# Pooled attention and a token and channel mixer on one core: another order of work, 16 heads with a ones column, results scaled on ScalarE

## The chip, the core and the metric

One core of a Trainium2 chip runs the whole program. The metric is the device time of one execution in microseconds; the kernel before has a median of 934.5 us over 3 runs (934.42 to 937.92).

## What is computed

The reference, cut to its core (4 batches, 8 heads, 1152 keys, head size 64; queries are averaged in pairs, so 576 of them):

```python
q_pool = q.reshape(B, H, S // 2, 2, D).mean(axis=3)
scores = 1.0 / np.sqrt(D) * np.matmul(q_pool, k.transpose(0, 1, 3, 2))
attn = np.exp(scores - np.max(scores, axis=-1, keepdims=True))
attn = attn / (np.sum(attn, axis=-1, keepdims=True) + 1e-09)
x = np.matmul(attn, v)                    # heads side by side: (4, 576, 512)
h = np.maximum(x.transpose(0, 2, 1) @ w_tok1, 0.0) @ w_tok2   # token mix, 576 -> 256 -> 576
u = x + h.transpose(0, 2, 1)
out = u + np.maximum(u @ w_ch1, 0.0) @ w_ch2                  # channel mix, 512 -> 1536 -> 512
```

## The kernel before, in words

Precision is kept by splitting each fp32 operand into a high part, rounded to the matmul's fp32r type, and a low part, the rest; products are sums of two or three matmuls. The work has three stages.

**Attention**, head by head, 32 heads. Per pair of heads, keys and pooled queries are loaded and turned by TensorE (`prep_kq`, lines 571 to 644), and copied to high and low tiles KHI, KLO, QHI, QLO. `stack` (lines 657 to 675) then makes, with DMAs from SBUF to SBUF, the stacked operands of a head: QQ holds the high queries twice (two transfers), KK the high keys over the low keys (two transfers, the last from `kl`), and K2 and Q2 the high keys and low queries for the rest of the product, with one more row for the maximum. `maxima` (lines 677 to 729) multiplies QQ by KK, 12 or 15 blocks per head on line 726, and VectorE reduces each block to row maxima on line 728; turned and sent by a small DMA, they become the last row of Q2, so that the score matmuls (line 791) subtract them. `main` (lines 770 to 850) takes nine steps per head: scores into one of two PSUM buffers "s", then ScalarE takes the exponential twice, to fp32 (`pf`, line 803) and to fp32r (`ph`, line 806), and GpSimd or VectorE takes the difference `pl` (line 810). The value matmuls of line 835 multiply ph and pl by V, whose high and low parts stand side by side.

The denominator has two ways. A head in the list `IN_PV` (line 94) has a column of ones next to V's high part, so the sum of the exponentials comes out as a 65th row; that takes three value matmuls per key block and half of the queries instead of two, 18 more per head. Another head has VectorE sum `pf` over the keys in three cuts per half, six per head (line 817), and `finish` turns those sums by five more transposes (line 881) and reduces them (lines 885, 888); it also adds V's two halves (line 848). `finish` (lines 852 to 905) turns the results, takes the reciprocal on VectorE and scales the results into U with two VectorE instructions (lines 900, 903).

**Token mix** per batch and half of the channels (`token_mix`), among the heads that follow. **Channel mix** (`make_ut`, `mm3`, `mm4`) at the end.

The order of each engine's instructions comes from a planner. Each `step` names an engine, a cost in ns, what it reads and writes, and a due time. `Plan.run` (lines 166 to 238) simulates the engines: of all steps that are ready it takes the one that can start first, and among equals the one due first. The order that it finds is the order of issue in the program; on the chip each engine runs its instructions in that order and waits on semaphores. Due times come from the table `DUE` (lines 33 to 91), as offsets in steps of the main loop. All transfers are issued on SP's queue. For them the planner has a common wire: a transfer is on it for its bytes at 360 GB/s (`wire`, line 337), not sooner than 1400 ns after its issue, and ends 900 ns later:

```python
            if s.eng == DMA:
                clock[DMA] = start + 650
                wire = max(start + 1400, wire) + s.cost
                s.end = wire + 900
```

A step with a second engine (`other`, as for pl: GpSimd first, VectorE as the other) is given to the other when the first would end more than `stay` ns later (line 195).

Of the kernel before, what the change touches and what calls it, by code (L numbers as in the profile page):

```python
# [33 lines left out]
    "scores": -1.44,  # L34
    "p_lo": 1.22,
    "sum": -6.47,
    "pv": 2.05,
    "o": -15.19,
    "finish": 7.6,
    "max": -29.13,  # L40
    "max_each": 0.09,
    "prep": -32.24,
    "v": 5.77,
    "stack": 7.14,
    "stack_2": 14.79,
    "mix": 9.79,
    "mix_x": 5.86,
    "w_tok": 0.59,
    "w_tok_each": 7.04,
    "w_bits": -43.21,  # L50
    "sum_each": 2.0,
    "pv_lo": -0.75,
    "lo_first": 70.21,
    "max_first": 50.9,
    "max_second": 0.54,
    "scores_each": -12.27,
    "p_hi": 0.25,
    "pv_one": -0.26,
    "finish_each": -35.22,
    "den_sum": -68.64,  # L60
    "x_lo": 7.7,
    "x": 8.02,
    "den": -16.32,
    "rd": -25.43,
    "u": -61.47,
    "u_each": 32.06,
    "max_of": 6.21,
    "max_row": -89.36,
    "max_first_each": 23.6,
    "q_pool": -42.98,  # L70
    "q_turn": 1.33,
    "k_each": 2.83,
    "k_hi": -30.98,
    "k_lo": 37.53,
    "q_hi": -105.28,
    "q_lo": -23.66,
    "load_kq": -1.52,
    "load_v": -98.6,
    "v_lo": -15.06,
    "load_w_tok": 1.53,  # L80
    "mix_x_lo": -8.66,
    "mix_1": 3.35,
    "mix_t": -0.86,
    "mix_2": 2.41,
    "mix_u": -20.08,
    "w_ch": 22.41,
    "w_ch_each": 12.8,
    "ut_0": -1.45,
    "ut_1": 1.58,
    "stay": 135.0,  # L90
# [3 lines left out]
IN_PV = (0, 1, 2, 3, 4, 5, 7, 9, 11, 12, 13, 15, 16, 18, 19, 21, 22, 23, 25, 27, 28, 31)  # L94
# [15 lines left out]
class Plan:  # L110
# [55 lines left out]
    def run(self):  # L166
# [17 lines left out]
        while len(order) < len(self.steps):  # L184
# [34 lines left out]
            if s.eng == DMA:  # L219
                clock[DMA] = start + 650  # L220
                wire = max(start + 1400, wire) + s.cost
                s.end = wire + 900
            else:
                s.end = clock[s.eng] = start + s.cost
                if s.shared:
                    port = s.end
# [15 lines left out]
def kernel(  # L242
# [24 lines left out]
    P = 128  # L267
# [31 lines left out]
    def f(t):  # L299
        return t.bitcast(F32)  # L300
# [137 lines left out]
    for i in range(2):  # L438
        ve.memset(f(K2[i])[D:D + 1, :], -1.0)
        ve.memset(DEN[i], 1.0)  # L440
    ve.memset(f(MH), 0.0)
    for i in range(2):
        po.memset(f(VV[i])[:, :, P:P + 1], 1.0)
        po.memset(OT[i], 0.0)
# [101 lines left out]
    def load_kq(p, t, after):  # L546
# [24 lines left out]
    def prep_kq(p, t):  # L571
# [10 lines left out]
        def keys(j):  # L582
            ps = Buf("s" if p == 0 else "r")
# [22 lines left out]
        def queries(i):  # L606
            c0, c1 = ((0, 3), (3, 5))[i]
            ps = Buf("s" if p == 0 else "r")
# [21 lines left out]
            if i == 1:  # L630
                for j in range(2):
                    r = slice(j * D, (j + 1) * D)
                    step(ACT, act_ps(REM),
                         lambda ps=ps, r=r, j=j, n=n: sc.copy(
                             QD[p % 2][r, j * REM:(j + 1) * REM], bank(ps)[r, n - REM:n]),
                         tq + 1.1 + due["q_hi"], [ps], [("qd", p % 2, j)])
# [20 lines left out]
    def stack(h, t, t2):  # L657
# [3 lines left out]
        for half, dst, src, n, read in (  # L661
# [3 lines left out]
            step(DMA, wire(4 * D * n),  # L665
# [11 lines left out]
    def maxima(h, t):  # L677
# [23 lines left out]
        step(DMA, 6, lambda: sy.dma_start(row[:, 0:4 * P], mt[0:4]), t,  # L701
             [("mt", h % 2)], [("row", h % 2, c) for c in range(4)])
        if h > 1:
            step(DMA, 6, lambda: sy.dma_start(
# [3 lines left out]
    def maximum(h, c, n, t):  # L708
# [15 lines left out]
        if h == 1 or h == 0 and c > 2:  # L724
            read.append(("m0", 2))
# [11 lines left out]
    def first_maxima(cs, t):  # L737
# [19 lines left out]
        step(PE, len(cs) * TURN, turn, t, [("m0", c) for c in range(cs[-1] + 1)], [ps], [ps])  # L757
# [12 lines left out]
    def main(h, t0):  # L770
# [8 lines left out]
        for s in range(NS):  # L779
# [3 lines left out]
            for i, (fq, c) in enumerate(units):  # L783
# [5 lines left out]
                def scores(st=st, i=i, fq=fq, c=c, terms=terms):  # L789
# [32 lines left out]
            for i, (fq, c) in enumerate(units):  # L822
# [16 lines left out]
                if c == NK - 1:  # L839
# [6 lines left out]
                    step(ACT, 415, lambda o=o, qs=qs: sc.copy(  # L846
# [5 lines left out]
    def finish(h, t):  # L852
# [25 lines left out]
        if not pv:  # L878
# [20 lines left out]
        r = rows(4)  # L899
        step(DVE, dve(4 * D), lambda: ve.tensor_mul(  # L900
            u[:, c0:c0 + 4, col], turned()[:, 0:4, 0:D], rd[:, 0:4].to_broadcast([P, 4, D])),
            t + due["u"], [*keys, ("rd", i2)], [*[("u", b, c, hh) for c in range(4)], *stage])
        step(DVE, 260, lambda: ve.tensor_mul(
            u[r, 8, col], turned()[r, 4, 0:D], rd[r, 4].to_broadcast([REM, D])),
            t + due["u"] + due["u_each"], [*keys, ("rd", i2)], [("u8", b // 2, hh), *stage])
# [282 lines left out]
```

## Time and profile before

| | us |
|---|---|
| median of 3 runs | 934.5 |
| the profiled execution | 931.58 |
| its span, first to last instruction | 929.8 |
| TensorE busy (matmuls) | 883.9 |
| VectorE busy | 635.0 |
| ScalarE busy | 520.4 |
| GpSimd busy | 331.6 |

The first head's work up to its first exponential ends at about 23 us, and the channel mixer fills the time from about 613 us on. A busy time counts the length of each instruction's record, without counting an overlap twice; matmuls follow each other faster than one record is long, so the pace of a row of matmuls is read from a run of them in the chain, not from the mean of one. In the rows below PE is TensorE, PEld its weight loads, DVE VectorE, ACT ScalarE, POOL GpSimd and SPq the issuing of transfers; "out<-in" are tile names with their numbers left out.

### The profile page before, as it was taken

The numbers are of one execution on the slowest core, as the hardware profiler recorded it, in microseconds if no ns is written. First come the engines' busy times: TensorE is split into PE (matmuls) and PEld (weight loads), VectorE is DVE, ScalarE is ACT, GpSimd is POOL, SyncE is SP. The second block draws the span as 40 slices with busy tenths as digits, with TensorE's granted clock in tenths as the row PEclk, the third lists the DMA queues.
The fourth block names the chain that finished last, engine by engine and source line by source line (L and its number), as shares of the span: only waits on it lengthen the run. The fifth ranks groups of instructions, "written<-read, shape, count | busy, mean of one in ns | idle before, by whom it ended". The sixth has DMA issues, their size and how long they took to land.

```text
span 929.8 us, 15513 instructions
## 1 busy us (share of the span) xinstructions
PE 883.9 (95%) x5679; PEld 817.7 (88%) x5679; DVE 635.0 (68%) x1291; ACT 520.4 (56%) x1040; POOL 331.6 (36%) x273
## 2 busy tenths in 40 slices
PE   7999999999999999989999999999999999999997
PEld 5888898888898899988998898989999999999996
DVE  7597888888888889887788998988882222221211
ACT  2878877768778678666777778854431111111110
POOL 2889747276345255374144735420000000000000
PEclk9999999999999999999999999999999999999999
DMA  6966653536546545644463435034420101000001
GB/s 165 257 148 159 155 126 91 128 94 150 135 96 153 135 97 131 142 98 108 100 150 75 107 71 135 24 113 137 137 91 1 69 1 34 1 35 1 35 1 35
DMA packets 89684, 91.09 MB, mean 98 GB/s; under 512 B 43852, under 2 KB 68808, under 8 KB 89608
## 3 DMA queue, kind: packets, MB, share of 16 engines
q1 hardware_dynamic: 89608, 90.09, 39.5%
q8 instruction: 45, 0.74, 0.3%
q14 instruction: 31, 0.25, 0.1%
HBM read 43.25 MB, written 4.72 MB: 52 GB/s over the span
## 4 chain that ended last, share of the span: by engine, by line
PE 71%; DMA 10%; ACT 7%; DVE 6%; SPq 4%; issue 2%; DVEq 0%; ACTq 0%; POOL 0%; POOLq 0%
PE r L1049 16%; PE o L835 13%; PE s L1077 13%; PE s L791 11%; DMA kk<-kl 10%; PE r L726 7%; PE o L1077 3%; ACT pf L803 3%; ACT ph L806 2%; SPq L666 2%; DVE mx L728 2%; PE r L934 2%; PE r L588 1%; PE r L952 1%; PE r L1077 1%
## 5 line engine op out<-in xcount | busy, mean ns | idle before, releaser
L810 POOL TENSOR_TENSOR pl<-pf,ph 128x576 fp32r<-128x576 f32 x170 | 245.4, 1459 | 189.0 <-ACT ph L806 94.0
L803 ACT ACTIVATE pf<-s 128x576 f32<-128x576 f32 x288 | 201.2, 700 | 121.3 <-PE s L791 115.5
L835 PE MATMUL o<-ph,vv 128*64 128x288 f32 (+2 forms) x972 | 211.5, 299 | 1.2 <-ACT ot L842 1.1
L728 DVE TENSOR_REDUCE mx<-r 128x1 f32<-128x384 f32 x384 | 189.2, 547 | 29.7 <-PE r L726 28.8
L806 ACT ACTIVATE ph<-s 128x576 fp32r<-128x576 f32 x288 | 186.7, 649 | 2.0 <-PE s L791 1.2
L791 PE MATMUL s<-qq,kk 128*128 128x288 f32 x574 | 169.4, 306 | 3.4 <-ACT ph L806 3.3
L791 PE MATMUL s<-q,k 65*128 65x288 f32 x576 | 166.2, 299 | 0.2 <-ACT q L760 0.2
L1057 DVE SCALAR_TENSOR_TENSOR h<-r,h 128x384 fp32r<-128x384 f32 x72 | 40.1, 557 | 168.4 <-ACT h L1055 167.8
L726 PE MATMUL r<-kk,qq 128*128 128x384 f32 x372 | 124.8, 352 | 30.5 <-DMA kk<-kl 26.0
L1055 ACT ACTIVATE h<-r 128x384 fp32r<-128x384 f32 x72 | 35.4, 491 | 195.9 <-PE r L1049 195.9
L835 PEld LDWEIGHTS o<-ph,vv 128*64 128x64 f32 (+2 forms) x972 | 136.5, 146 | 6.4 <-ACT ot L842 2.2
L835 PE MATMUL o<-pl,vv 128*65 128x288 f32 (+1 forms) x576 | 140.0, 300 | 0.8 <-POOL pl L810 0.5
L1077 PE MATMUL s<-w,h 128*128 128x512 f32 x504 | 130.9, 394 | 0.0
L791 PEld LDWEIGHTS s<-qq,kk 128*128 128x128 f32 x574 | 109.9, 192 | 9.0 <-ACT ph L806 6.9
L791 PEld LDWEIGHTS s<-q,k 65*128 65x128 f32 x576 | 110.6, 192 | 0.5 <-ACT q L760 0.5
L810 DVE TENSOR_TENSOR pl<-pf,ph 128x576 fp32r<-128x576 f32 x118 | 92.7, 787 | 24.5 <-ACT ph L806 19.5
L1049 PE MATMUL r<-big,w 128*128 128x384 f32 x576 | 108.8, 337 | 0.0
L1077 PEld LDWEIGHTS s<-w,h 128*128 128x128 f32 x504 | 93.4, 188 | 16.6
L1049 PEld LDWEIGHTS r<-big,w 128*128 128x128 f32 x576 | 101.7, 188 | 3.7 <-DVE big L1038 0.2
L726 PEld LDWEIGHTS r<-kk,qq 128*128 128x128 f32 x372 | 69.6, 192 | 39.6 <-issue 23.3
L835 PEld LDWEIGHTS o<-pl,vv 128*65 128x65 f32 (+1 forms) x576 | 83.4, 153 | 3.9 <-POOL pl L810 1.8
L817 DVE TENSOR_REDUCE sum<-pf 128x96 f32<-128x960 f32 x60 | 67.7, 1138 | 0.8 <-ACT pf L803 0.4
(132 smaller groups left out, 1094.5 us busy)
## 6 DMA issues: line engine op xcount, KB each, us to landing
raw<-in_moe_w_ch_dram SPq DMA_DIRECT2D x24, 512.0 KB
kk<-kh SPq DMA_DIRECT2D x32, 288.0 KB
qq<-qh SPq DMA_DIRECT2D x64, 144.0 KB
kk<-kl SPq DMA_DIRECT2D x32, 288.0 KB
vn<-in_v_dram SPq DMA_DIRECT2D x32, 288.0 KB
k<-kk SPq DMA_DIRECT2D x31, 288.0 KB
kn<-in_k_dram SPq DMA_DIRECT2D x30, 288.0 KB
qn<-in_q_dram SPq DMA_DIRECT2D x32, 256.0 KB
```

The costliest lines, as they stand in the source:

```text
L726: step(PE, mm(SP3), lambda ps=ps, w=w, x=x: te.matmul(at(ps)[:, 0:SP3], w, x, start=True, stop=True), t, read, [ps], [ps])
L728: step(DVE, dve(SP3), lambda ps=ps, m=m: ve.tensor_reduce(m, at(ps)[:, 0:SP3], axis=AX.X, op=ALU.max), t + due["max_of"], [ps], [key])
L791: te.matmul(at(st)[:, i, 0:HF], w[:, c * P:(c + 1) * P], x[:, fq * HF:(fq + 1) * HF], start=(n == 0), stop=(n == len(terms) - 1))
L803: step(ACT, act_ps(2 * HF), lambda pf=pf, st=st: sc.activation(pf, at(st)[:, :, 0:HF], AF.Exp, scale=ESC), t, [(st, 0), (st, 1)], [("pf", s)])
L806: step(ACT, act_ps(2 * HF), lambda ph=ph, st=st: sc.activation(at(ph), at(st)[:, :, 0:HF], AF.Exp, scale=ESC), t + due["p_hi"], [(st, 0), ...
L810: both(2 * HF, lambda e, pf=pf, ph=ph, pl=pl: e.tensor_sub(at(pl), pf, f(at(ph))), t + due["p_lo"], [("pf", s), ph], [pl], [pl], on=POOL i ...
L817: step(DVE, 65 + 1.06 * (NK + 1) * HF // CUT, lambda fq=fq, cs=cs: ve.tensor_reduce(SUM[:, fq, cs], PF[:, fq, :, cs].rearrange("p c x i -> ...
L835: lambda o=o, x=x, w=w, m=m, i=i, c=c, new=new, end=end: te.matmul(at(o)[0:m - w], VV[i2][:, c, w:m], at(x)[:, i], start=new, stop=end),
L1049: te.matmul(at(ps)[:, 0:GT], w[:, c], x[:, c], start=(c == 0 and n == 0), stop=(c == NC4 - 1 and n == 2))
L1055: step(ACT, act_ps(GT), lambda: sc.activation(at(h)[:, 0], at(ps)[:, 0:GT], AF.Relu), t, [ps], [h])
L1057: step(DVE, dve(GT), lambda: ve.scalar_tensor_tensor(out=at(h)[:, 1], in0=at(ps)[:, 0:GT], scalar=0.0, in1=f(at(h))[:, 0], op0=ALU.max, op ...
L1077: te.matmul(at(ps), a[:, x * P:(x + 1) * P], w, start=(fi == 0 and m == 0), stop=(fi == NF - 1 and m == 2))
```

## The change

- **Durations of transfers.** The planner's figures for transfers become longer on the wire (factors of 1.3 to 1.85 for the stacked operands and their copies, 1.4 for query loads) with shorter fixed ends (1265 and 650 ns); the small transfers of the maxima count 1 ns of wire, not 6. Two costs of ScalarE steps are changed as well (the small query copy 230, and pf 49 ns dearer where it is written with gaps).
- **The due times** in `DUE` are all others, and `stay` is 800, not 135. The order of nearly every instruction and transfer can differ.
- **`IN_PV`** has 16 heads, not 22. In these heads pf is written contiguously, except in the middle one of the nine steps.
- **Scaling.** The closing results are scaled by ScalarE, five instructions per head with a scale read per partition, where VectorE had two.
- **First head.** The key row of -1 is filled by ScalarE, not VectorE; two GpSimd fills of OT are left out; of its five turns of keys and queries two use the "s" buffers and three the ring "r", where all five used "s". A step of the maxima waits in the plan for the turn of the first three, not for the third of them.

The diff, cut:

```diff
 DUE = {
...
-    "max": -29.13,
+    "max": -26.45,
...
-    "stack": 7.14,
-    "stack_2": 14.79,
+    "stack": 10.93,
+    "stack_2": 29.0,
...
-    "stay": 135.0,
+    "stay": 800,
 }
-IN_PV = (0, 1, 2, 3, 4, 5, 7, 9, 11, 12, 13, 15, 16, 18, 19, 21, 22, 23, 25, 27, 28, 31)
+IN_PV = (0, 1, 2, 3, 5, 8, 10, 13, 15, 19, 21, 24, 26, 28, 29, 31)
...
-                wire = max(start + 1400, wire) + s.cost
-                s.end = wire + 900
+                wire = max(start + 1265, wire) + s.cost
+                s.end = wire + 650
...
-        ve.memset(f(K2[i])[D:D + 1, :], -1.0)
+        sc.activation(K2[i][D:D + 1, :], ident[D:D + 1, 0:1].to_broadcast([1, S]), AF.Copy,
+                      bias=-1.0, scale=0.0)
...
-        po.memset(OT[i], 0.0)
...
-            step(DMA, wire(4 * 2 * n * (c1 - c0) * D), lambda: sy.dma_start(
+            step(DMA, 1.4 * wire(4 * 2 * n * (c1 - c0) * D), lambda: sy.dma_start(
...
-            ps = Buf("s" if p == 0 else "r")
+            ps = Buf("s" if p == 0 and j == 0 else "r")
...
-            ps = Buf("s" if p == 0 else "r")
+            ps = Buf("s" if p == 0 and i == 0 else "r")
...
-            step(DMA, wire(4 * D * n),
+            step(DMA, (1.3 if dst is QQ else 1.8) * wire(4 * D * n),
...
-        step(DMA, wire(4 * D * S), lambda: sy.dma_start(f(K2[h % 2])[0:D], f(KK[i])[0:D]),
+        step(DMA, 1.85 * wire(4 * D * S), lambda: sy.dma_start(f(K2[h % 2])[0:D], f(KK[i])[0:D]),
...
-        step(DMA, wire(4 * D * SQ),
+        step(DMA, 1.7 * wire(4 * D * SQ),
...
-            pf = (PF[:, 0, s].rearrange("p x i -> p i x") if s < NK // 2
-                  else PF[:, :, NK // 2, :, 0] if s == NK // 2
-                  else PF[:, 1, s - NK // 2 - 1].rearrange("p x i -> p i x"))
-            step(ACT, act_ps(2 * HF), lambda pf=pf, st=st: sc.activation(
+            pv = h in IN_PV
+            half, x = (0, s) if s < NK // 2 else (1, s - NK // 2 - 1)
+            near = pv and s != NK // 2
+            pf = (PF[:, :, NK // 2, :, 0] if s == NK // 2
+                  else PF[:, half, x].rearrange("p x i -> p (x i)").rearrange("p (i x) -> p i x", i=2) if near
+                  else PF[:, half, x].rearrange("p x i -> p i x"))
+            step(ACT, act_ps(2 * HF) + (0 if near else 49), lambda pf=pf, st=st: sc.activation(
...
-        step(DVE, dve(4 * D), lambda: ve.tensor_mul(
-            u[:, c0:c0 + 4, col], turned()[:, 0:4, 0:D], rd[:, 0:4].to_broadcast([P, 4, D])),
...
-        step(DVE, 260, lambda: ve.tensor_mul(
-            u[r, 8, col], turned()[r, 4, 0:D], rd[r, 4].to_broadcast([REM, D])),
...
+        for c in range(NQ):
+            r, row, out_ = ((slice(0, P), c0 + c, ("u", b, c, hh)) if c < 4
+                            else (rows(4), 8, ("u8", b // 2, hh)))
+            step(ACT, 230 if c > 3 else 140, lambda c=c, r=r, row=row: sc.mul(
+                u[r, row, col], turned()[r, c, 0:D], rd[r, c]),
+                t + due["u"] + due["u_each"] * (c > 3), [(ps, 0, c), ("rd", i2)], [out_, *stage])
```

## Rows read from the trace of the kernel before

**Rows 1.** Busy time by stage, whole span (columns named in its first line).

```profile
core 0: us, PE busy (x) PEld busy (x) DVE busy (x) ACT busy (x) POOL busy (x), PEclk, DMA share, GB/s
0.00:23.00 23.00, 17.14 (x69) 11.85 (x70) 16.90 (x44) 4.98 (x11) 5.02 (x16) 0.99 0.69 165
23.00:613.00 590.00, 555.59 (x4010) 524.00 (x4009) 497.90 (x1028) 447.04 (x895) 324.81 (x256) 0.99 0.52 122
613.00:929.80 316.80, 311.21 (x1603) 281.83 (x1601) 120.18 (x222) 68.39 (x135) 1.77 (x1) 1.00 0.15 49
```

**Rows 2.** Who waited for whom, whole span: us in total, times, longest us.

```profile
ACT pf L803 <- PE s L791: 115.5, 109, 3.3
...
PE r L726 <- DMA kk<-kl: 26.0, 19, 2.6
...
PEld s L791 <- ACT ph L806: 6.9, 16, 0.8
...
PE r L726 <- DVE mx L728: 2.1, 4, 1.0
```

**Rows 3.** The chain that ended last, in order of time: start us, us, what.

```profile
126.01 0.66 PE r L588 x6
...
130.19 1.06 PE o L835 x8
...
172.04 5.98 DMA kk<-kl
...
470.44 4.07 DMA kk<-kl
```

**Rows 4.** Instructions in order of time, 131 to 146 us, SP and PE.

```profile
136.11 0.54 SPq L666 DMA_DIRECT2D kk<-kl  x1
...
141.74 0.74 PE L726 MATMUL r<-kk,qq 128*128 128x384 f32 x2 [1.83 <-DMA kk<-kl]
```

**Rows 5.** Busy time and granted clock (PEclk) around three stalls, columns as in rows 1.

```profile
142.00:146.00 4.00, 4.00 (x19) 4.00 (x19) 2.98 (x6) 1.74 (x3) 2.04 (x3) 0.57 0.28 78
...
398.00:402.00 4.00, 4.00 (x20) 4.00 (x19) 3.03 (x9) 2.08 (x5) 1.44 (x2) 0.57 0.03 8
...
23.00:27.00 4.00, 4.00 (x20) 3.90 (x19) 3.36 (x8) 3.48 (x6) 3.10 (x3) 0.63 1.24 220
```

**Rows 6.** Groups by line and shape: count, busy us, mean ns, idle before.

```profile
L810 POOL TENSOR_TENSOR pl<-pf,ph 128x576 fp32r<-128x576 f32 x170 | 245.4, 1459 | 189.0 <-ACT ph L806 94.0 <-PE o L835 51.0 <-DMA qq<-qh 13.8
L803 ACT ACTIVATE pf<-s 128x576 f32<-128x576 f32 x288 | 201.2, 700 | 121.3 <-PE s L791 115.5 <-DVE sum L817 3.9
L728 DVE TENSOR_REDUCE mx<-r 128x1 f32<-128x384 f32 x384 | 189.2, 547 | 29.7 <-PE r L726 28.8
L806 ACT ACTIVATE ph<-s 128x576 fp32r<-128x576 f32 x288 | 186.7, 649 | 2.0 <-PE s L791 1.2
...
L810 DVE TENSOR_TENSOR pl<-pf,ph 128x576 fp32r<-128x576 f32 x118 | 92.7, 787 | 24.5 <-ACT ph L806 19.5 <-issue 2.1 <-PE s L791 0.9
...
L817 DVE TENSOR_REDUCE sum<-pf 128x96 f32<-128x960 f32 x60 | 67.7, 1138 | 0.8 <-ACT pf L803 0.4
...
L900 DVE TENSOR_TENSOR u<-r,rd 128x256 f32<-128x256 f32 x32 | 13.4, 418 | 0.4
...
L848 DVE TENSOR_TENSOR ot<-o,low 64x288 f32<-64x288 f32 x20 | 8.9, 446 | 4.9 <-ACT low L846 4.4
...
L903 DVE TENSOR_TENSOR u<-r,rd 64x64 f32<-64x64 f32 x32 | 7.3, 228 | 0.7
...
L885 DVE TENSOR_REDUCE r<-r 128x4 f32<-128x512 f32 x10 | 7.0, 696 | 2.3 <-PE r L881 2.2
...
L634 ACT CAST qd<-r 64x64 fp32r<-64x64 f32 x30 | 6.5, 218 | 0.6 <-DVE ql L638 0.4
```

**Rows 7.** Instructions in order of time, first 24 us, DVE, PE and ACT.

```profile
1.81 1.02 DVE L439 MEMSET k<- 1x1152 f32 x1 [0.28 <-issue]
...
6.60 0.52 PE L614 MATMUL s<-ident,qp 128*128 128x128 f32 x3 [0.49 <-DVE identr L375]
...
7.15 0.48 ACT L628 CAST qh<-s 128x384 fp32r<-128x384 f32 x1 [5.14 <-PE s L614]
```

More of the change, by code (lines that the diff above doesn't have):

```diff
@@ L33 @@
 DUE = {
[L34 to L39, printed above, removed]
-    "max": -29.13,
-    "max_each": 0.09,
-    "prep": -32.24,
-    "v": 5.77,
-    "stack": 7.14,
-    "stack_2": 14.79,
[L46 to L89, printed above, removed]
-    "stay": 135.0,
+    "scores": -2.94,
+    "p_lo": 5.94,
+    "sum": -8.53,
+    "pv": 1.65,
+    "o": -51.23,
+    "finish": 9.59,
+    "max": -26.45,
+    "max_each": 0.91,
+    "prep": -32.39,
+    "v": 3.41,
+    "stack": 10.93,
+    "stack_2": 29.0,
+    "mix": 4.49,
+    "mix_x": 5.65,
+    "w_tok": 9.27,
@@ new lines @@
+    "w_tok_each": 4.51,
+    "w_bits": -133.66,
+    "sum_each": 0.15,
+    "pv_lo": 0.35,
+    "lo_first": -20.44,
+    "max_first": 50.63,
+    "max_second": 6.11,
+    "scores_each": -5.89,
+    "p_hi": -0.31,
+    "pv_one": 0.14,
+    "finish_each": -4.69,
+    "den_sum": -16.19,
+    "x_lo": -25.04,
+    "x": 38.5,
+    "den": -32.79,
+    "rd": -22.19,
+    "u": 15.67,
+    "u_each": -29.42,
+    "max_of": -7.63,
+    "max_row": -47.64,
+    "max_first_each": 17.12,
+    "q_pool": -5.06,
@@ L91 @@
+    "q_turn": 3.94,
+    "k_each": 1.81,
+    "k_hi": -2.71,
+    "k_lo": 5.81,
+    "q_hi": -15.06,
+    "q_lo": 47.2,
+    "load_kq": -51.29,
+    "load_v": -22.47,
+    "v_lo": -60.85,
+    "load_w_tok": -81.39,
+    "mix_x_lo": -54.2,
+    "mix_1": 3.42,
+    "mix_t": 0.6,
+    "mix_2": 3.13,
+    "mix_u": -133.49,
+    "w_ch": 91.67,
+    "w_ch_each": 17.54,
+    "ut_0": -21.58,
+    "ut_1": -34.33,
+    "stay": 800,
 }
-IN_PV = (0, 1, 2, 3, 4, 5, 7, 9, 11, 12, 13, 15, 16, 18, 19, 21, 22, 23, 25, 27, 28, 31)
+IN_PV = (0, 1, 2, 3, 5, 8, 10, 13, 15, 19, 21, 24, 26, 28, 29, 31)
@@ L632, in queries @@
                     r = slice(j * D, (j + 1) * D)
-                    step(ACT, act_ps(REM),
+                    step(ACT, 230,
                          lambda ps=ps, r=r, j=j, n=n: sc.copy(
@@ L700, in maxima @@
         row = f(Q2[h % 2])[D:D + 1]
-        step(DMA, 6, lambda: sy.dma_start(row[:, 0:4 * P], mt[0:4]), t,
+        step(DMA, 1, lambda: sy.dma_start(row[:, 0:4 * P], mt[0:4]), t,
              [("mt", h % 2)], [("row", h % 2, c) for c in range(4)])
         if h > 1:
-            step(DMA, 6, lambda: sy.dma_start(
+            step(DMA, 1, lambda: sy.dma_start(
                 row[:, 4 * P:SQ], MT[0][4:5, j * REM:(j + 1) * REM]), t,
@@ L724, in maximum @@
         if h == 1 or h == 0 and c > 2:
-            read.append(("m0", 2))
+            read.append(("m0", "turned"))
         step(PE, mm(SP3), lambda ps=ps, w=w, x=x: te.matmul(
@@ L755, in turn @@
                     at(ps)[0:D + 1, x * P:(x + 1) * P], M0[:, c:c + D + 1], ident)
-        step(PE, len(cs) * TURN, turn, t, [("m0", c) for c in range(cs[-1] + 1)], [ps], [ps])
+        step(PE, len(cs) * TURN, turn, t, [("m0", c) for c in range(cs[-1] + 1)],
+             [ps, *([("m0", "turned")] if cs[0] == 0 else [])], [ps])
         n = (len(cs) if 4 not in cs else 1.5) * P
@@ L845, in main @@
                         continue
-                    step(ACT, 415, lambda o=o, qs=qs: sc.copy(
+                    step(ACT, 420, lambda o=o, qs=qs: sc.copy(
                         LOW[:, qs], at(o)[D:P]), t + due["o"], parts, [("low", fq)])
@@ L898, in finish @@
         stage = [("stage",)] if b >= 2 else []
-        r = rows(4)
-        step(DVE, dve(4 * D), lambda: ve.tensor_mul(
-            u[:, c0:c0 + 4, col], turned()[:, 0:4, 0:D], rd[:, 0:4].to_broadcast([P, 4, D])),
-            t + due["u"], [*keys, ("rd", i2)], [*[("u", b, c, hh) for c in range(4)], *stage])
-        step(DVE, 260, lambda: ve.tensor_mul(
-            u[r, 8, col], turned()[r, 4, 0:D], rd[r, 4].to_broadcast([REM, D])),
-            t + due["u"] + due["u_each"], [*keys, ("rd", i2)], [("u8", b // 2, hh), *stage])
+        for c in range(NQ):
[4 more added lines that the diff above has]
+                t + due["u"] + due["u_each"] * (c > 3), [(ps, 0, c), ("rd", i2)], [out_, *stage])
     def token_mix(b, i, t):
```

## The prediction

> **What bounds the kernel now.** I read the busy times by stage first, then the waits, then the chain that ended last, and last the instructions around one stall. By stage [rows 1] the run falls into a start of 23 us, an attention stage of 590 us and the channel mixer of 316.8 us. In the mixer TensorE is busy 311.2 of 316.8 us, so nothing that the change touches there can give much. In the attention stage it is busy 555.6 of 590, VectorE 497.9, ScalarE 447.0 and GpSimd only 324.8. These are averages; the waits say which comes last. TensorE's one large wait is for the last transfer of a head's stacked operands (kk from kl, issued on line 666), ahead of the maxima matmuls of line 726: 26.0 us in 19 waits [rows 2]. Its other waits are small: 2.1 us for VectorE's maxima reductions, and its weight loads 6.9 us for ScalarE's exponentials. The other way round, ScalarE waits 115.5 us for scores. So the stage follows TensorE's queue, and the queue is held mainly by a transfer.
>
> Why it is held can be seen around 141 us [rows 4]. The kl transfer is issued at 136.11; TensorE works off what the plan put ahead of the maxima, then stands for 1.83 us until the matmul of 141.74. The chain shows 18 such pieces from issue to landing, 4.07 to 5.98 us, 4.9 in the mean [rows 3]. The planner's figures for the same come out of its code. Four transfers (qq, qq, kh, kl) are issued 0.65 us apart, so kl at 1.95; wire times are 0.41, 0.41, 0.82 and 0.82 us, the first starts after 1.4, and 0.9 is added: kl ends at 5.24, 3.3 us after its issue (3.5 with a k2 copy queued ahead). The trace is 1.5 us longer in the mean, and 26.0/19 = 1.4 us is the mean wait. The order believes in a landing that comes later than planned.
>
> **The change, part by part.**
>
> Durations of transfers. With the new factors (1.3 for qq, 1.8 for kk, 1.85 and 1.7 for the copies, 1.265 and 0.65 us for the ends) the same four take 0.53, 0.53, 1.47 and 1.47 us of wire, and kl ends at 6.17, 4.2 us after its issue, or 5.1 with the k2 copy (1.52) ahead. That lies across the 4.07 to 5.98 of the trace. So the maxima should move about 1 to 1.6 us back in TensorE's queue, with scores and value matmuls ahead of them. Bounds: nothing gained, if the plan has no other work for that time, or all 26.0. I take two thirds, **-17.3 us**: the new figure still lies below the longest landings, and the order is fixed before the run. Next late is then the 6.9 us behind the exponentials.
>
> Clock. TensorE was granted 0.57 of its clock from 142 to 146 us and from 398 to 402, and 0.63 from 23 to 27 [rows 5], which is 1.2 GHz for most of it instead of 2.4; the first of them comes right behind the stall of 141 us. Each cost 0.37 to 0.43 x 4 = 1.5 to 1.7 us. Bounds 0 to -5.1 for the three; with shorter stalls I take two of three, **-3.4 us**.
>
> Heads with ones. Such a head spends a third value matmul per key block, 18 a head. Six heads fewer are 108 matmuls at 1.06/8 = 0.1325 us [rows 3], -14.3 us; each then has five more transposes of its sums, 30 at 0.66/6 = 0.11 us, +3.3. Both are on TensorE's path: **-11.0 us**.
>
> VectorE pays for that [rows 6]: per converted head six sums of 1.138 us, a reduction of 0.696 and one of a quarter of that width (about 0.2, an estimate from the same row), and two additions of 0.446: 8.6 us, 52 in all. It is relieved of the scaling, 32 x (0.418 + 0.228) = 20.7 us. Net +31 us on a queue busy 497.9 of 590. Its cover is the larger "stay": a low part (pl) goes to VectorE only where GpSimd would end 800 ns later, not 135. VectorE does 118 of them at 0.787; 40 moved away pay for the 31 us, and cost GpSimd 40 x 1.459 = 58 us of the 265 it has idle. What is queued behind the sums on VectorE are maxima reductions, and TensorE waits for those through three banks. If the cover fails, this is the slower rival below.
>
> ScalarE gets five scaled copies per head, 160 in all. The nearest row is the 64x64 copy on line 634, 0.218 us: 35 us, 1.1 a head. They wait for VectorE's reciprocal, with exponentials queued behind them, and scores wait for those. Against it the contiguous pf in heads with ones costs 0.649, not 0.700 [rows 6], for 8 of 9 steps of 16 heads: -6.5 us. So ScalarE goes from 447 to about 476 of some 560 us: no bound in the mean. For these two engines together I put **+2 us** on the path; bounds -5 (VectorE's queue gets shorter if over 40 pl move) and +34 (all scaled copies exposed).
>
> On the ScalarE copies the trace of before shows no copy whose scale is read per partition. The Trainium skill ("ScalarE: Activation LUTs", "What ACT_TABLE_LOAD costs") says that each such pointer operand adds about 93 ns, and its "Rules for kernel authors" give multiplications to VectorE. By that figure the 160 copies would be 15 us dearer, and the +2 would be nearer +10. No run so far shows it.
>
> First head. Two fills of 1.02 us leave VectorE, which did the identity cast that the first transposes wait 0.49 us for [rows 7]; the two fills take their place on ScalarE, which is idle for 5.14 us there. The key and query turns no longer share two banks. Bounds -2.0 (the fills) and +1.5 (the ring's three banks are those of the first maxima); I take **-1 us**.
>
> Other due times, and with them the order of every DMA on SP's queue, move too; SP issues in order, so a transfer placed behind one that waits is late itself. I price that at nothing and leave it in the range.
>
> **Sum**: -17.3 - 3.4 - 11.0 - 1 + 2 = -30.7 us against the profiled execution's 931.6 (span 929.8, 1.8 around it), so 900.9. That execution lies 2.9 us below the median of 934.5, so in medians 903.8, say **904 us**.
>
> **The rivals.**
>
> First, the waits stay. If the maxima have nothing to change places with, or transfers later in the queue are pushed back as far, only the matmuls are gained: 934.5 - 11 = 923 us. For it: the plan is an estimate for transfers that also meet loads from DRAM. Against it: the shortfall of 1.5 us and the mean wait of 1.4 agree.
>
> Second, VectorE decides, and the kernel gets **slower**. The place: each half of a converted head, where three sums, 3.4 us, stand ahead of maxima reductions on its queue. Three banks of the ring cover about two reductions, 2 x 0.547 = 1.1 us [rows 6], so up to 2.3 us of wait per half, 12 x 2.3 = 28 us, less 11 for the matmuls: about 951 us if the stack waits also stay. It decides from 0.9 us per half on, where the 11 us are eaten, plus what the stack waits return. Against it: the ten such heads of before left only 2.1 us of waits for those reductions [rows 2], and GpSimd has room.
>
> Third, ScalarE decides: the 35 us of copies fall where the exponentials are late already and are exposed almost whole, so the gain is given back: 934.5 - 30.7 - 2 + 34 = 936 us. The engine is idle for 143 of the 590 us, mostly waiting for scores, which speaks against it. The rule of the Trainium skill given above ("ScalarE: Activation LUTs", "Rules for kernel authors") would point here.
>
> Fourth, everything comes: all stack waits, all clock drops, pl moved freely: -26 - 5.1 - 11 - 2 - 5 = -49, or 885 us.
>
> That the change doesn't do what it says can't quite be excluded: landings of 6 us would still be late by the new figures, which is inside the first rival.
>
> **How the numbers follow.** Forecast (890 to 918) 0.52, waits stay 0.17, VectorE decides 0.10, ScalarE decides 0.10, everything comes 0.11. A measurement of this kernel tells about 0.5% from no change, 4.7 us; faster means under 929.8. The forecast and the fourth rival are faster, and most of the first (0.13) and a little of the third (0.02): 0.78. Same: the rest of the first and most of the third, 0.10. Slower: 0.12. The range goes from the fourth rival's 885 to 931, which holds the first, and leaves out VectorE's case and most of ScalarE's, near 2 in 10.
>
> **What would show it.** The waits of line 726 for kk should fall from 26.0 to some 9 us; line 835 should have 108 matmuls fewer; sums should be 96, not 60; pl on VectorE should be under 80, and TensorE's granted clock should dip once at most inside the attention stage, which should last about 560 us. The prediction is wrong if waits for maxima reductions or exponentials appear on TensorE by tens of microseconds, or if the mixer is no longer at 316.8.

## The result, and the profile after

The kernel after takes 923.1 us (920.0 to 923.9, 4 runs), the kernel before beside it 934.6: a ratio of 0.9863, interval 0.9831 to 0.9895. That is 1.4% faster, small but clear of its interval. 923.1 lies inside the range, but the gain is 11.5 us between the medians (12.8 by the ratio) where the sum had 30.7.

By stage, columns as in [rows 1], for the kernel after:

```profile
0.00:23.00 23.00, 18.66 (x86) 13.89 (x86) 16.33 (x44) 11.58 (x21) 8.34 (x17) 1.00 0.72 163
23.00:613.00 590.00, 567.86 (x3967) 523.03 (x3967) 462.83 (x915) 487.61 (x1058) 476.95 (x379) 0.99 0.53 124
613.00:920.80 307.80, 303.01 (x1551) 274.37 (x1549) 111.52 (x185) 62.95 (x123) 26.68 (x19) 1.00 0.14 45
```

The span is 9.0 us shorter. In the same 590 us VectorE is busy 35 us less, ScalarE 41 us more and GpSimd 152 us more. The cut at 613 us now falls later in the program's work: the last value matmul ends at 605.3 us before and at 596.0 us after, which leaves 324.5 and 324.8 us to the end. So the whole gain lies ahead of the mixer.

Who waited for whom, kernel after, whole span (us, times, longest), against [rows 2]:

```profile
ACT ph L810 <- PE s L792: 38.9, 55, 3.1
...
PEld s L792 <- ACT pf L807: 12.3, 28, 0.9
...
ACT u L906 <- DVE rd L899: 9.5, 7, 2.1
...
PE s L792 <- ACT pf L807: 5.3, 17, 0.7
...
PEld r L726 <- DVE mx L728: 4.9, 16, 1.3
...
PE r L726 <- DVE mx L728: 1.5, 2, 1.1
...
PE r L726 <- DMA q<-ql: 1.2, 1, 1.2
```

And two more of the kernel before:

```profile
PEld r L726 <- DVE mx L728: 6.0, 13, 1.2
...
PE s L791 <- ACT ph L806: 3.3, 10, 0.5
```

The 26.0 us behind kk are gone; TensorE's longest wait for any transfer is 1.2. The largest entries are now many waits of half a microsecond for ScalarE's exponentials: 5.3 us on matmuls and 12.3 on weight loads, where it was 3.3 and 6.9 (the two overlap and can't be added). TensorE's idle time, span less busy time, went from 45.9 to 31.3 us. ScalarE waits 38.9 us for scores, not 115.5 (in front of ph, which now comes first).

Groups by line and shape, kernel after, against [rows 6]:

```profile
L814 POOL TENSOR_TENSOR pl<-pf,ph 128x576 fp32r<-128x576 f32 x264 | 377.4, 1447 | 93.2 <-ACT pf L807 38.9 <-PE o L839 31.1 <-ACT u L906 3.8
...
L821 DVE TENSOR_REDUCE sum<-pf 128x96 f32<-128x960 f32 x96 | 108.0, 1141 | 1.5 <-ACT pf L807 1.2
...
L906 ACT ACTIVATE u<-r,rd 128x64 f32<-128x64 f32 x128 | 34.2, 319 | 7.7 <-DVE rd L899 6.1 <-PE r L955 1.0
...
L814 DVE TENSOR_TENSOR pl<-pf,ph 128x576 fp32r<-128x576 f32 x24 | 23.7, 988 | 22.6 <-ACT ph L810 11.8 <-PE o L839 5.6 <-PE s L792 3.1
...
L906 ACT ACTIVATE u<-r,rd 64x64 f32<-64x64 f32 x32 | 9.9, 309 | 4.1 <-DVE rd L899 3.4
```

Sums are 96, as worked out; subtractions on VectorE went from 118 to 24, more than the 40 I counted on. Two stretches of the kernel after at half clock, columns as above:

```profile
32.00:38.80 6.80, 5.85 (x22) 4.72 (x23) 3.80 (x11) 5.73 (x13) 5.51 (x5) 0.51 0.66 171
451.70:455.10 3.40, 3.40 (x15) 3.40 (x16) 3.11 (x6) 0.97 (x2) 1.45 (x1) 0.50 1.01 224
```

At 0.51 and 0.50 they lose some 3.3 and 1.7 us, 5.0 together, against 3 x 1.5 to 1.7 before [rows 5].

### The profile page after: what moved, and what is told of

It reads as the page before. It is cut to its first block, busy times and chain, and to the rows that moved or that the text cites. A ratio compares the mean times of both kernels' runs of the same rounds, so it can differ in the third digit from the quotient of the medians.

```text
span 920.8 us, 15741 instructions
## 1 busy us (share of the span) xinstructions
PE 889.5 (97%) x5601; PEld 811.3 (88%) x5601; DVE 590.7 (64%) x1142; ACT 562.1 (61%) x1202; POOL 512.0 (56%) x414
## 4 chain that ended last, share of the span: by engine, by line
PE 75%; ACT 10%; DVE 5%; issue 2%; DMA 1%; POOL 1%; SPq 0%; ACTq 0%; DVEq 0%; POOLq 0%
PE r L1052 17%; PE o L839 14%; PE s L1080 13%; PE s L792 12%; PE r L726 7%; ACT pf L807 3%; ACT ph L810 3%; PE o L1080 3%; PE r L937 2%; PE r L955 2%; PE r L877 2%; DVE mx L728 1%; PE r L885 1%; ACT u L906 1%; PE r L588 1%
## 5 line engine op out<-in xcount | busy, mean ns | idle before, releaser
L814 POOL TENSOR_TENSOR pl<-pf,ph 128x576 fp32r<-128x576 f32 x264 | 377.4, 1447 | 93.2 <-ACT pf L807 38.9
L728 DVE TENSOR_REDUCE mx<-r 128x1 f32<-128x384 f32 x384 | 197.4, 548 | 41.6 <-PE r L726 37.9
L810 ACT ACTIVATE ph<-s 128x576 fp32r<-128x576 f32 x288 | 187.6, 655 | 50.8 <-PE s L792 38.9
L807 ACT ACTIVATE pf<-s 128x576 f32<-128x576 f32 x288 | 194.2, 680 | 9.4 <-POOL pl L814 7.1
L839 PE MATMUL o<-ph,vv 128*65 128x288 f32 (+2 forms) x864 | 186.9, 302 | 3.9 <-ACT ot L846 1.4
L839 PE MATMUL o<-pl,vv 128*65 128x288 f32 (+1 forms) x576 | 135.7, 297 | 0.2 <-POOL pl L814 0.2
L839 PEld LDWEIGHTS o<-ph,vv 128*65 128x65 f32 (+2 forms) x864 | 125.7, 155 | 11.1 <-DVE ot L852 3.0
L726 PE MATMUL r<-kk,qq 128*128 128x384 f32 x372 | 127.1, 361 | 6.7 <-DMA q<-ql 1.2
L792 PEld LDWEIGHTS s<-qq,kk 128*128 128x128 f32 x574 | 109.4, 191 | 14.9 <-ACT pf L807 12.3
L821 DVE TENSOR_REDUCE sum<-pf 128x96 f32<-128x960 f32 x96 | 108.0, 1141 | 1.5 <-ACT pf L807 1.2
L839 PEld LDWEIGHTS o<-pl,vv 128*65 128x65 f32 (+1 forms) x576 | 88.1, 163 | 1.8 <-POOL pl L814 0.6
L1015 POOL TENSOR_TENSOR w<-v,w 128x512 fp32r<-128x512 f32 x23 | 32.1, 1396 | 58.1 <-ACT w L1014 58.1
```

The costliest lines, as they stand in the source:

```text
L726: step(PE, mm(SP3), lambda ps=ps, w=w, x=x: te.matmul(at(ps)[:, 0:SP3], w, x, start=True, stop=True), t, read, [ps], [ps])
L728: step(DVE, dve(SP3), lambda ps=ps, m=m: ve.tensor_reduce(m, at(ps)[:, 0:SP3], axis=AX.X, op=ALU.max), t + due["max_of"], [ps], [key])
L792: te.matmul(at(st)[:, i, 0:HF], w[:, c * P:(c + 1) * P], x[:, fq * HF:(fq + 1) * HF], start=(n == 0), stop=(n == len(terms) - 1))
L807: step(ACT, act_ps(2 * HF) + (0 if near else 49), lambda pf=pf, st=st: sc.activation(pf, at(st)[:, :, 0:HF], AF.Exp, scale=ESC), t, [(st, ...
L810: step(ACT, act_ps(2 * HF), lambda ph=ph, st=st: sc.activation(at(ph), at(st)[:, :, 0:HF], AF.Exp, scale=ESC), t + due["p_hi"], [(st, 0), ...
L814: both(2 * HF, lambda e, pf=pf, ph=ph, pl=pl: e.tensor_sub(at(pl), pf, f(at(ph))), t + due["p_lo"], [("pf", s), ph], [pl], [pl], on=POOL i ...
```

## The experiments

| kernel | median us | ratio to before, interval |
|---|---|---|
| after | 923.1 | 0.9863 (0.9831 to 0.9895) |
| e1 before + transfer durations | 922.3 | 0.9858 (0.9801 to 0.9915) |
| e6 e1, additions on GpSimd | 913.2 | 0.9759 (0.9719 to 0.9799) |
| e14 e6, price 800 | 911.3 | 0.9720 (0.9664 to 0.9776) |
| e18 e14, all subtractions on GpSimd | 915.0 | 0.9765 (0.9724 to 0.9806) |
| e17 e1 + due times and price 800 | **908.3** | 0.9710 (0.9684 to 0.9736) |
| e8 after, 22 heads with ones | 923.8 | 0.9877 (0.9832 to 0.9923) |
| e16 after, 22 heads, price 135 | 938.1 | 1.0019 (0.9990 to 1.0047) |
| e11 after, price 135 | 950.7 | 1.0128 (1.0095 to 1.0162) |
| e13 e11, short sums | 941.6 | 1.0048 (1.0021 to 1.0075) |
| e7 before, 16 heads | 966.5 | 1.0339 (1.0280 to 1.0399) |
| e10 e6, 16 heads | 947.9 | 1.0097 (1.0061 to 1.0134) |
| e15 e14, 16 heads | 931.0 | 0.9932 (0.9902 to 0.9961) |
| e2 after, scaling on VectorE, order held | 926.0 | 0.9890 (0.9831 to 0.9949) |
| e3 after, token weights loaded elsewhere | 920.1 | 0.9822 (0.9774 to 0.9871) |
| e4 after, short sums, order held | 921.2 | 0.9830 (0.9782 to 0.9878) |
| e5 after, halved subtractions, order held | 918.2 | 0.9805 (0.9765 to 0.9845) |
| e9 e2, e4 and e5 at once | 910.6 | 0.9703 (0.9665 to 0.9742) |
| e12 after, first head as before | 921.3 | 0.9809 (0.9777 to 0.9841) |

"Order held" means that a step does other work under its old cost in the plan, so that each queue keeps its order; elsewhere the plan is made anew. The intervals of e9, e14 and e17 overlap, so which of the three is fastest is not known.

### The transfers alone, and what VectorE then waits for

**e1** has the new transfer durations and nothing else.

```diff
-                wire = max(start + 1400, wire) + s.cost
-                s.end = wire + 900
+                wire = max(start + 1265, wire) + s.cost
+                s.end = wire + 650
...
-            step(DMA, wire(4 * D * n),
+            step(DMA, (1.3 if dst is QQ else 1.8) * wire(4 * D * n),
...
```

> The kernel before with nothing but the new durations of transfers in its planner (its own due times, 22 heads with ones, scaling on VectorE). If the stack waits were worth themselves, as the prediction took it, the waits of line 726 for kk fall from 26.0 us to under 9 and the time falls by 17 to 26 us, to 909 to 917. If a planner that knows the longer transfers only spreads the same wait over others (the rival of the waits that return elsewhere), the waits for kk vanish too, but the time falls by 0 to 10 us, to 924 to 934, and TensorE's waits for ScalarE and VectorE grow by 10 us or more.

922.3 us, between the two theories: this part alone gives as much as the whole change. Its waits on TensorE (us, times, longest):

```profile
PE r L726 <- DVE ql L638: 9.8, 3, 4.6
...
PE r L726 <- DMA kk<-kl: 1.2, 4, 0.4
```

The 26.0 us behind kk became 1.2, and 9.8 behind ql are new. Instructions of e1 in order of time (start us, us) show one of them:

```profile
139.01 4.88 DVE L577 TENSOR_TENSOR qp<-qn 128x256 f32<-128x256 f32 x1
143.93 0.82 DVE L638 TENSOR_TENSOR ql<-r,qh 128x384 fp32r<-128x384 f32 x2
...
139.40 4.21 POOL L810 TENSOR_TENSOR pl<-pf,ph 128x576 fp32r<-128x576 f32 x3
...
144.54 1.01 PE L726 MATMUL r<-kk,qq 128*128 128x384 f32 x2 [4.55 <-DVE ql L638]
```

An addition that takes 0.53 us in the median of e1's 18 takes 4.88: it ends at 143.89, 0.28 us after the last of three of GpSimd's subtractions that run back to back. Both engines' steps read two operands from SBUF. The Trainium skill ("SBUF — State Buffer", "Who interferes with whom") says that a VectorE instruction with two SBUF inputs contends with a GpSimd instruction that reads SBUF, over ports that it calls an exclusive lock; the trace agrees, and the loser here waits for a run of three. Behind it ql is late, TensorE stands, and a stretch at half clock follows. It happens again at 285.50 (4.85 us). The two stretches:

```profile
142.40:149.20 6.80, 4.66 (x18) 4.59 (x19) 6.61 (x10) 1.25 (x3) 2.65 (x2) 0.50 0.96 229
289.10:295.90 6.80, 4.91 (x19) 4.84 (x20) 6.50 (x10) 1.23 (x2) 2.42 (x2) 0.50 0.92 221
```

**e6** holds e1's order and issues the additions of line 577 on GpSimd.

```diff
-            both(n, lambda e, r=r, c0=c0, c1=c1: e.tensor_add(
+            both(n, lambda e, r=r, c0=c0, c1=c1: (po if p else e).tensor_add(
```

> The kernel before with the new transfer durations alone (922.3 us), its order held, but each query-pair addition that the order put on VectorE issued on GpSimd instead, from the second pair on. There one VectorE addition of two SBUF operands took 4.88 us, usually 0.5, while three GpSimd subtractions ran back to back, and TensorE waited 9.8 us in 3 waits for the ql behind it, with two stretches of half clock following. Theory A (VectorE is shut out by GpSimd at the SBUF, and that gives back the stack waits' gain): the 9.8 us of waits and at least one of the two half-clock stretches go, 907 to 914. Rival B (the late qp is late for another reason, or moves to GpSimd's queue): 918 to 926.

913.2 us, theory A. Its waits, and its attention in the columns of the stages:

```profile
PE r L726 <- DVE mx L728: 3.3, 8, 0.8
...
PE r L726 <- DVE ql L638: 1.1, 2, 0.8
```

```profile
23.00:602.00 579.00, 563.82 (x4049) 525.88 (x4048) 507.34 (x1030) 450.06 (x901) 329.30 (x270) 1.00 0.53 126
```

The ql waits fall from 9.8 to 1.1 us, and with them both half-clock stretches go: the granted clock is 1.00 throughout the attention. In the kernel before, the longest of VectorE's 23 additions took 1.70 us, so e6 mends a stall that e1's order had brought, not an old one.

### The heads with ones

**e7**: before with the new list alone. **e8**: after with the old list.

```diff
-IN_PV = (0, 1, 2, 3, 4, 5, 7, 9, 11, 12, 13, 15, 16, 18, 19, 21, 22, 23, 25, 27, 28, 31)
+IN_PV = (0, 1, 2, 3, 5, 8, 10, 13, 15, 19, 21, 24, 26, 28, 29, 31)
```

> The kernel before with 16 heads with ones in place of 22, all else as before, the order made anew. TensorE's work shrinks by 108 matmuls of 0.1325 us less 30 transposes of 0.11, some 11 us. Theory A (the work taken off TensorE comes back whole as waits, because TensorE already waits for the others in the stages): within 3 us of before, 931 to 938. Rival B (the work is saved as I forecast): 921 to 928, with the kk waits of 26 us still there.

> The kernel after with before's 22 heads with ones, the order made anew. Theory A (fewer heads with ones load VectorE and GpSimd so that TensorE's waits fill what was saved): TensorE's work grows by 11 us and its waits shrink by as much, 920 to 926. Rival B (the 16 heads do save their 11 us, and the waits of the kernel after have another cause): 930 to 938.

e7 took 966.5 us, which neither theory had: six heads fewer cost some 30 us with the old due times. e8 took 923.8, A's figure: with and without 11 us of TensorE's work the time is the same. Where the kernel after loses them is seen in part only: TensorE's idle time is 31.3 us, 30.2 in e8, and its half-clock stretch at 451.7 (1.7 us) is not in e8's trace. The rest must lie in the spacing of matmuls, which a busy time doesn't show; no run here tells what sets it.

**e11** sets the price back in the kernel after; **e10** puts 16 heads into e6.

```diff
-    "stay": 800,
+    "stay": 135,
```

> The kernel after with the planner's price for moving a subtraction to VectorE put back from 800 to 135, the order made anew: some 100 of the 264 subtractions go from GpSimd (1.447 us each) to VectorE (0.8 to 1.0). Theory A (GpSimd's load is what makes TensorE's short waits in the kernel after, as the halved subtractions' 5 us say): 915 to 920. Rival B (VectorE, with 96 sums, then is late with the row maxima instead): 925 to 935.

> The kernel with the transfer durations and the additions on GpSimd (913.2 us) and 16 heads with ones for its 22, the order made anew. TensorE's work shrinks by 10.7 us. Theory A (fewer heads with ones come back whole as waits, as between the kernel after and its copy with 22): 910 to 920, TensorE's idle time in the attention up by 8 us or more. Rival B (with the stack waits and VectorE's blocked additions gone the saved work shows): 900 to 906.

950.7 and 947.9 us, both above anything expected. e11's wait for row maxima (from 23 to 640 us), and where its subtractions went:

```profile
PE r L726 <- DVE mx L728: 9.9, 11, 3.5
...
PEld r L726 <- DVE mx L728: 17.7, 32, 3.8
```

```profile
L814 POOL TENSOR_TENSOR pl<-pf,ph 128x576 fp32r<-128x576 f32 x210 | 307.1, 1476 | 203.5 <-ACT pf L807 69.3 <-PE o L839 58.5 <-PE r L726 27.3
...
L814 DVE TENSOR_TENSOR pl<-pf,ph 128x576 fp32r<-128x576 f32 x78 | 63.8, 820 | 12.9 <-ACT pf L807 6.7 <-PE s L792 4.2 <-PE o L839 0.8
```

54 subtractions more on VectorE, and the matmuls' wait for its maxima rises from 1.5 to 9.9 us. Whether that is VectorE's work or an order with due times fitted to 800, **e13** asks: e11, order held, each sum over one pair of five.

```diff
-                        PF[:, fq, :, cs].rearrange("p c x i -> p x c i"),
+                        PF[:, fq, 0:1, cs].rearrange("p c x i -> p x c i"),
```

> The kernel after with the price at 135 (950.7 us), its order held, each sum over one pair of five (the rest of the denominators' terms left out), some 70 us less of VectorE's work. Theory A (VectorE's work, the 96 sums on top of 78 subtractions, is what TensorE waits for there): 932 or less. Rival B (the order, made with due times fitted to the price of 800, is what is slow): 943 or more.

941.6 us, between the two: a third of the 27 us (9.1) goes with VectorE's work. The rest is not its load as a whole, since with the short sums VectorE is busy 589.9 us, as in the kernel after (590.7); it lies in the order, and in part in the clock (below). **e14**, **e15** and **e16** fill the table (the same two edits).

> The kernel with the transfer durations and the additions on GpSimd (913.2 us, 22 heads, price 135) with the price at 800, the order made anew. Theory A (VectorE's load is the matter at either count of heads, so moving some 100 subtractions to GpSimd helps): 905 to 911. Rival B (with 60 sums VectorE has room, and GpSimd at 1.46 us a subtraction is slower than VectorE at 0.8): 914 to 922.

> The same with 16 heads with ones and the price at 800 (947.9 us at 135). Theory A (the 35 us that 16 heads cost there are VectorE's load, which the price of 800 takes away): 905 to 922. Rival B (due times fitted to 22 heads): 935 or more.

> The kernel after with 22 heads with ones and the price at 135 (923.8 us with 22 at 800, 950.7 us with 16 at 135), the order made anew. Theory A (with 60 sums VectorE has room for the subtractions again): 915 to 930. Rival B (these due times need the price of 800, whatever the count of heads): 940 or more.

| | 22 heads | 16 heads |
|---|---|---|
| e6's due times, 135 | 913.2 | 947.9 |
| e6's due times, 800 | 911.3 | 931.0 |
| after's due times, 135 | 938.1 | 950.7 |
| after's due times, 800 | 923.8 | 923.1 |

e14, e15 and e16 lie between their two theories, e14 within 0.3 us of A. Sixteen heads gain in no row. The price of 800 is worth 17 and 28 us with 16 heads, 2 and 14 with 22. With the due times of the kernel after it keeps the 16 heads from being a loss; with e6's they lose 20 us even so.

Part of these losses is TensorE's clock. The mean granted clock of each profiled execution, times its span, gives an estimate of what half clock cost:

| step | loss, us | mean granted clock | of the loss, by the clock |
|---|---|---|---|
| before to e7 | 32 | 0.993 to 0.980 | 13 |
| e6 to e10 | 35 | 0.999 to 0.989 | 10 |
| after to e11 | 28 | 0.994 to 0.986 | 8 |
| e8 to e16 | 14 | 0.995 to 0.986 | 8 |
| e14 to e15 | 20 | 0.997 to 0.998 | none |

e14 shows the block at the SBUF once more, now of a subtraction (order of time):

```profile
212.15 4.63 DVE L810 TENSOR_TENSOR pl<-pf,ph 128x576 fp32r<-128x576 f32 x1
...
211.93 4.22 POOL L810 TENSOR_TENSOR pl<-pf,ph 128x576 fp32r<-128x576 f32 x3
...
216.83 0.53 PE L835 MATMUL o<-pl,vv 128*128 128x288 f32 x2 [3.35 <-DVE pl L810]
```

**e18** issues all of e14's subtractions on GpSimd (po in place of e on line 810, order held).

> The kernel with the durations, the additions on GpSimd and the price of 800 (911.3 us), its order held, with the 28 subtractions that the order still gives VectorE issued on GpSimd. One of them took 4.63 us on VectorE while GpSimd worked; TensorE then waited 3.4 us and a half-clock stretch of 3.4 us followed. Theory A (VectorE shut out by GpSimd): 905 to 909. Rival B (the 28 at 1.46 us in GpSimd's queue make other waits as long): 910 to 916.

915.0 us, in rival B's range, though its interval overlaps e14's. The 3.4 us are gone, but a wait for maxima of 3.7 us came (its sum 5.6, 1.8 in e14), and weight loads wait 8.8 us for pl (3.8 in e14):

```profile
PE r L726 <- DVE mx L728: 5.6, 5, 3.7
...
PEld o L835 <- POOL pl L810: 8.8, 24, 1.0
```

### The engines' loads in the kernel after

All with the order held: **e2** scales on VectorE, four chunks in one step; **e4** shortens the sums as in e13; **e5** halves the subtractions from the third head on (its edit is shown, cut); **e9** does all three.

```diff
+            w = slice(0, 2 if h < 2 else 1)
...
-                at(pl), pf, f(at(ph))), t + due["p_lo"], ...
+                at(pl)[:, w], pf[:, w], f(at(ph))[:, w]), t + due["p_lo"], ...
```

> The changed kernel with the order of all its steps held as it is, but the closing results scaled by VectorE at the same places (two instructions a head, five in each fourth head). If ScalarE's 160 copies expose their time (the third rival), the time falls by 10 us or more from 923, to 913 or less, and the waits of scores for pf shrink. If they are covered, as the prediction took it, the time stays within 3 us of 923.

> The changed kernel, order held, with each VectorE sum over pf taken over one key block pair of five, so that it is some 0.3 us long instead of 1.14 (the denominators of the 16 heads without ones leave out four fifths of their terms). That takes about 80 us of work off VectorE. If VectorE's sums hold the maxima reductions and through them TensorE (the second rival), the time falls by 10 us or more, to 913 or less. If GpSimd's taking of pl has made room for them, it stays within 4 us of 923.

> The kernel after with its order held, each closing subtraction pf - ph from the third head on over one of its two units alone (the other half of pl keeps older values, so the result isn't the attention's). GpSimd's 1.45 us steps should come down to about 0.75, its busy time in the attention from 477 to about 310 us. Theory A (TensorE's many short waits in the kernel after come from GpSimd, 81% busy and slow for each subtraction): at least 5 us faster than after's 923, 918 or less. Rival B (GpSimd is covered as VectorE's sums and ScalarE's copies were, and the short waits are the order's own): within 3 us of after, 920 to 926.

> The kernel after with its order held and three loads cut at once: the closing results scaled by VectorE (ScalarE's share), each sum over one pair of five, each subtraction over one unit of two from the third head on; the last two leave out terms of the denominators and of the results. Alone they gave +3, -2 and -5 us. Theory A (the many short waits in the kernel after, some 2 us a head, are the order's: what stands next on TensorE is often not yet ready, whatever the load of the others): 912 to 919, little more than the subtractions alone. Rival B (any one engine's relief is taken over by the next loaded one, and the three together are what TensorE waits for): below 908.

926.0, 921.2, 918.2 and 910.6 us. Taking ScalarE's copies away gains nothing, the shorter sums 2 us, GpSimd's halved subtractions 5 (the row below: 858 ns in the mean, 1447 in the kernel after); the interval of each overlaps that of the kernel after, so none is shown to gain alone. All three together give 12.5 us, clear of noise, between e9's two theories and nearer A. That is more than the three alone add up to (4 us), so in part one engine's relief is taken over by the next, as rival B has it. Yet e9 is no faster than e17, below, with all its work (0.9703 and 0.9710), so another order and another split of the same work get as far without taking any away.

```profile
L815 POOL TENSOR_TENSOR pl<-pf,ph 128x288 fp32r<-128x288 f32 (+1 forms) x264 | 225.1, 858 | 200.1 <-ACT pf L807 105.5 <-PE o L840 33.8 <-ACT ph L810 21.8
```

### The start, and the due times

**e3** loads the token weights at other due times; **e12** puts the first head's steps back on their engines and banks.

```diff
-    "w_bits": -133.66,
+    "w_bits": -10,
...
-    "load_w_tok": -81.39,
+    "load_w_tok": -30,
```

```diff
-        sc.activation(K2[i][D:D + 1, :], ident[D:D + 1, 0:1].to_broadcast([1, S]), AF.Copy,
-                      bias=-1.0, scale=0.0)
+        ve.memset(f(K2[i])[D:D + 1, :], -1.0)
...
-            ps = Buf("s" if p == 0 and j == 0 else "r")
+            ps = Buf("s" if p == 0 else "r")
...
```

> The changed kernel with two due times altered, so that the token weights are loaded behind the next pair's keys and queries and their bit steps come later (load_w_tok -30, w_bits -10; the order after the first heads is nearly the same). If the first two heads lost their time to those loads and the steps that wait for them, the first exponential of head 2 comes at 60 to 64 us, not 69.4, and the time falls by 5 to 9 us, to 914 to 918. If the start is slow for another reason, head 2 stays at 67 to 70 and the time within 3 us of 923.

> The kernel after with the first head's steps back on the engines and banks of before (the rows of -1 written by VectorE, all first transposes in the scores' banks, the old order of the first maxima's turns), due times as in after. Theory A (these moves are what costs the 8 us that heads 0 to 2 lose): 915 to 919, the third head's first exponential before 66 us. Rival B (the due times of the first steps and a half-clock stretch of 6.8 us cost it, not the engines): within 3 us of 923.

920.1 and 921.3 us; both intervals overlap that of the kernel after, so neither accounts for its late start. Head 2's first exponential, the 19th pf, starts at 61.09 us before, 69.38 after, and still at about 68.0 and 69.0 in these two. **e17** has the due times and the price beside the durations, and the rest of before.

```diff
-    "scores": -1.44,
+    "scores": -2.94,
...
-    "stay": 135.0,
+    "stay": 800,
...
```

> The kernel before with the new transfer durations and the new due times (the price of 800 among them), its 22 heads, its first head and its VectorE scaling kept. Theory A (the due times put other work ahead of head 2 and cost the start): head 2's first exponential at 66 us or later, the whole at 920 to 928, as the kernel after with 22 heads (923.8). Rival B (ScalarE's scaling or the first head's moves cost the start after all): head 2 at 62 to 64 us as with the durations alone, the whole at 912 to 919.

908.3 us, the lowest median, 2.9% below before, and neither theory's pair: head 2 is as late as A had it (the row below), the whole faster than B. So a late head 2 need not mean time lost.

```profile
68.22 0.69 ACT L803 ACTIVATE pf<-s 128x576 f32<-128x576 f32 x1
```

Waits for exponentials in e17, then in e8, which differs from e17 by the scaling on ScalarE, the layout of pf, ScalarE's new costs in the plan, and the first head's moves:

```profile
PE s L791 <- ACT pf L803: 4.0, 7, 0.9
...
PEld s L791 <- ACT pf L803: 9.3, 22, 1.1
```

```profile
PE s L792 <- ACT pf L807: 8.0, 14, 1.0
...
PEld s L792 <- ACT pf L807: 14.9, 26, 1.2
```

They are twice and half again as much, and e8 is 15.5 us slower. TensorE's idle time is 23.3 us in e17 and 30.2 in e8, and both have a mean granted clock of 0.995.

## Why the prediction was right in sign and wrong in size

e1, e17, e8 and after each add one part to the one before. Their ratios times 934.5 us are 921.2, 907.4, 923.0 and 921.7, so:

| part | forecast | measured step |
|---|---|---|
| durations (stack waits; clock) | -17.3, -3.4 | -13.3 |
| other due times, price | 0 | -13.8 |
| ScalarE's scaling with pf's layout and plan costs, first head | +2, -1 | +15.6 |
| six heads fewer with ones | -11.0 | -1.3 |
| sum | -30.7 | -12.8 |

The steps hang on this sequence, since every new order mixes the parts. In the first three the intervals on both sides of the step stand apart; the last does not differ from nothing.

**Durations**: right in mechanism and nearly in size. Nearly all of the kk waits went (1.2 us left in e1), not two thirds; 9.8 us came back behind a blocked addition, and with that mended the part gives 0.9759, or -22.5.

**Clock**: failed. Half clock lasts as long as before, 10.2 us, at other places. In e1 the stretches follow the new stalls of 4.5 us, and in e6, where the longest stall from 23 to 602 us is 1.15 us, there is none in that stretch. But a stall's length does not decide it: before, the longest stall of the attention (1.89 us, until 515.68) has no such stretch behind it, and the stretch at 451.7 us of the kernel after follows one of 0.79. So "two of three" was a guess.

**Other due times at nothing**: failed, and to the good. I left their whole effect to the range; in this sequence it is as large as that of the durations. Part of it is the gain of e6 once more: e17 has 43 of its 48 additions on GpSimd, e1 30, and no wait for ql of e1's length. Against e6 it has 4.6 us, with overlapping intervals. The price alone gives 2 us (e14).

**"For these two engines together I put +2 us on the path"**: failed. My bound of +34 held it, and the sign was that of the third rival. Its mechanism is seen in the kernel after, where ScalarE stands 9.5 us ahead of the scaled copies for VectorE's reciprocal (2.6 in e8), but not its price: e2 takes the copies off ScalarE with the order held and gains nothing (it puts 24 us of scaling on VectorE, and has 16 heads with ones, so it does not test e8's step itself). The copies take 44.1 us, not 35. The 64x64 copy takes 309 ns against 218 for the plain copy of that shape [rows 6], 91 more; the Trainium skill ("ScalarE: Activation LUTs", "What ACT_TABLE_LOAD costs") has about 93 for such an operand, and the trace agrees. What costs the 15.6 us is not shown. The order that the plan makes with these steps is likely, since no load was found that does it; but which of them changes it (the scaling, pf's layout, the plan's costs of 49, 230 and 420 ns, the last of which the list of the change leaves out) stays open. Only the first head's moves were undone alone, and they are worth little (e12).

**"Both are on TensorE's path: -11.0 us"**: failed. The work did shrink: TensorE has 78 records fewer, 5601 against 5679, which is 108 matmuls less and 30 transposes more. But e8, with the work put back, is as fast. In the 590 us VectorE is busy 78%, ScalarE 83 and GpSimd 81, and the time taken from TensorE's work did not leave the path. On other due times or at the other price the same step costs 13 to 35 us (the table). So the second rival named an engine that matters: e13 gives it 9.1 us. Its 951 is not far from e7's 966.5, but some 13 us of e7's loss are half clock, for which the 951 has no term, so the agreement is partly luck. The price of 800, which I took for its cover, is one with the due times of the kernel after (e11) and not with e6's (e15). My "only 2.1 us" of waits for the reductions was short as well: weight loads waited another 6.0 for them, partly at the same time.

**Of what I said would show it**: kk waits, sums, subtractions on VectorE and the matmul count came as said. The clock did not, and the attention became 9.3 us shorter, not 30. The waits for exponentials grew, in pieces of half a microsecond and by less than the tens that I had named as the sign of an error. The mixer is as long as before.

## What to carry to other kernels

When the longest wait of the bounding engine is removed, cost the rest of the change against the engines that were second, not against the bounding one alone: 11 us of matmuls saved were worth nothing here, and cost 13 to 35 us beside other settings. A kernel whose order is planned from costs has parts that fit only each other: test them in a ladder (one part more in each kernel), since the whole was worth 12 us here and its first two rungs 27. Before moving an elementwise step with two SBUF operands between VectorE and GpSimd, look for runs of such steps on the other engine.

## What was not expected of the hardware

A VectorE step with two SBUF operands, an addition of 0.53 us in the median or a subtraction of 0.79 in the mean [rows 6], lasted 4.88 and 4.85 us (e1) and 4.63 (e14) beside GpSimd. Each ended 0.3 to 0.6 us after three of GpSimd's subtractions that ran back to back, and these took 4.21/3 = 1.40 and 4.22/3 = 1.41 us each, no slower than in the mean. In e10 a subtraction took 4.93 us beside a run of five. It is rare: in e1, 35 of the 138 additions and subtractions on VectorE overlap GpSimd's work, and only these two take over 1.5 us. Why these lose several times in a row is not shown.
